# Five more satisfied wait instructions on SyncE ahead of the last store

## The chip, the cores and the metric

The kernel runs on one core of a Trainium2 chip. The metric is the device time of one execution in microseconds (us), lower is better. Each execution also has a span, from the first to the last instruction of the program.

## The reference, cut to what matters

The reference adds a linear-attention block with softmax feature maps and a SiLU feed-forward block, both fed by one layer norm, to their input of 2048 rows and 448 columns:

```python
def reference(A_x, A_wqkv, A_w_phi, A_wo, B_x, B_w1, B_w2):
    ...                                  # _A_ref: attention, _B_ref: SiLU feed-forward
    x = A_x
    xn = _layernorm(x, axis=-1)
    return x + _A_ref(xn, A_wqkv, A_w_phi, A_wo) + _B_ref(xn, B_w1, B_w2)
```

The change touches none of this arithmetic.

## The kernel before

The kernel records all its operations, puts them in order with its own scheduler and then emits each engine's stream. Every finished row tile of the result is stored from ScalarE's queue, except the second half of the very last tile, which SyncE stores. SyncE is the engine that in this program only issues transfers and waits. A wait is an instruction that holds its engine until a semaphore, a counter that engines and transfers raise, has reached a value; it is satisfied if the value was reached before. A store has landed when its data have arrived and its semaphore says so:

```python
P.op("dve", ..., lambda e: e.tensor_tensor(res[:, cs], ob, addend[:, cs], ALU.add), ..., name="out_ev")
P.dma(lambda e: e.dma_start(out=rows_of(out, t, t + 1)[:, 0, cs], in_=res[:, cs]), ..., name="out_dma",
      out_slot=ob_cnt[0] % NOS, eng="sp" if cs.start else "act")
```

This is the loop that emits an engine, SyncE among them. The last lines are SyncE's waits for all stores to have landed (NOS is 4):

```python
def emit_engine(ename, eng):
    waited = {}
    for oid in order[ename]:
        o = ops[oid]
        need = {}
        ...                                  # collects what o depends on
        for key, (sm, val) in need.items():
            if waited.get(key, 0) >= val:
                continue
            eng.wait_ge(sm, val)
            waited[key] = val
        ins = o.fn(eng)
        ...
    if ename == "sp":
        for i in range(NOS):
            if out_cnt[i] > 0:
                eng.wait_ge(out_sems[i], 16 * out_cnt[i])
```

SyncE's stream of the kernel before has 79 instructions. The last five are a transpose issue (75th), the wait for the last addition (76th), the store (77th) and two waits for the landings (78th and 79th).

The softmax here doesn't subtract the row's maximum and nothing guards it: scores larger than these inputs give would overflow.

## Time and profile before

| | before |
|---|---|
| time, first three runs | 149.09, 149.17 and 149.71 us |
| profiled run: time, span | 149.45 us, 147.6 us |
| TensorE busy | 143.4 us, 97% of the span |
| SyncE idle ahead of its last store | 9.5 us |
| last addition done, store issued, end of span | 145.98, 146.07, 147.6 us |

### The profile page before, as it was taken

The page shows a single profiled execution, that of the slowest core. Times are in us where ns is not written, and L with a number is a line of the kernel's source. Part 1 is how long each engine was busy: PE and PEld are TensorE (multiplying, and loading weights), DVE is VectorE, ACT ScalarE, POOL GpSimd, SP SyncE. Part 2 cuts the span into 40 slices and gives each one's busy share as a digit, 9 for nine tenths or more (in the row PEclk, how much of TensorE's full clock was granted, in tenths as well). Part 3 has the DMA queues.
Part 4 walks back from the last instruction along what each step waited for, and adds up shares of the span by engine and source line. Part 5 has one row for each costly group of instructions (what it writes and reads, how often), then busy time and mean ns, then how long its engine had stood idle before and what let it go on. Part 6 is the DMA issues. An engine that isn't in the chain of part 4 may idle for free.

```text
span 147.6 us, 3735 instructions
## 1 busy us (share of the span) xinstructions
PE 143.4 (97%) x1572; PEld 79.7 (54%) x1572; DVE 91.1 (62%) x196; ACT 71.8 (49%) x92; POOL 74.0 (50%) x92
## 2 busy tenths in 40 slices
PE   7989999999999999999999999999999999999994
PEld 7884444544544557655444455555555465555473
DVE  2958997190799889207993018969701958252383
ACT  4657675759994988998655597080000000000000
POOL 8618566501099999996999600983940000000000
PEclk9999999999999999999999999999999999999999
DMA  4999964899920000000387391079676925542154
GB/s 109 331 355 247 295 119 70 154 134 301 334 61 0 0 0 4 4 4 0 41 172 147 77 141 36 0 148 119 127 142 134 232 84 98 107 38 39 34 174 137
DMA packets 44496, 17.53 MB, mean 119 GB/s; under 512 B 37040, under 2 KB 44096, under 8 KB 44480
## 3 DMA queue, kind: packets, MB, share of 16 engines
q1 hardware_dynamic: 41648, 15.10, 50.5%
q10 hardware_dynamic: 2704, 2.17, 4.4%
q8 instruction: 12, 0.20, 0.6%
q0 software_dynamic: 128, 0.03, 0.1%
q14 instruction: 4, 0.03, 0.1%
HBM read 6.57 MB, written 1.84 MB: 57 GB/s over the span
## 4 chain that ended last, share of the span: by engine, by line
PE 92%; DMA 4%; SPq 1%; DVE 1%; issue 1%; ACT 0%
PE psum L482 91%; DMA phT<-in_B_w_dram 4%; SPq L516 1%; DVE x_sb L896 1%; DVE Wqk L636 0%; PE psum L497 0%; ACT last_lo L502 0%; ACT last_hi L502 0%
## 5 line engine op out<-in xcount | busy, mean ns | idle before, releaser
L482 PE MATMUL psum<-xnT,phT 64*128 64x512 bf16 (+1 forms) x428 | 45.6, 350 | 0.9 <-DMA phT<-in_B_w_dram 0.4
L482 PE MATMUL psum<-w_sb,hT 128*128 128x448 bf16 (+1 forms) x238 | 45.4, 341 | 0.0
L814 POOL TENSOR_TENSOR RA<-Ek_sb,Rec 128x896 bf16<-128x896 bf16 x16 | 27.0, 1721 | 13.1 <-DVE Rec L779 10.2
L502 ACT ACTIVATE hT<-psum 128x1024 bf16<-128x1024 f32 x28 | 27.3, 1024 | 12.8 <-PE psum L482 12.8
L778 DVE TENSOR_REDUCE Rec<-Ek_sb 128x32 f32<-128x896 bf16 (+1 forms) x20 | 24.4, 1252 | 14.4 <-POOL Ek_sb L509 7.5
L482 PEld LDWEIGHTS psum<-w_sb,hT 128*128 128x128 bf16 x238 | 22.2, 98 | 18.7 <-issue 1.1
L482 PEld LDWEIGHTS psum<-xnT,phT 64*128 64x128 bf16 (+1 forms) x428 | 21.0, 95 | 20.9 <-PE psum L482 0.6
L502 ACT ACTIVATE Ek_sb<-psum 128x864 bf16<-128x864 f32 x24 | 20.1, 910 | 7.1 <-POOL RA L814 4.4
L482 PE MATMUL psum<-Wqk,xnT 64*128 64x432 bf16 x224 | 23.4, 343 | 0.1
L874 DVE TENSOR_SCALAR den<-psum 128x16 f32<-128x16 f32 x16 | 2.3, 156 | 23.3 <-PE psum L482 23.3
L482 PEld LDWEIGHTS psum<-Wqk,xnT 64*128 64x128 bf16 x224 | 10.5, 94 | 10.1 <-issue 0.8
L788 POOL TENSOR_TENSOR Ek_sb<-Ek_sb,Rec 128x896 bf16<-128x896 bf16 x8 | 13.3, 1700 | 5.1 <-DVE Rec L779 5.1
L788 POOL TENSOR_TENSOR phT<-phT,Rec 128x896 bf16<-128x896 bf16 x8 | 13.3, 1702 | 0.0
L482 PE MATMUL psum<-wv,xnT 64*128 64x448 bf16 x112 | 12.9, 349 | 0.0
L643 DVE BATCH_NORM_STATS2 st<-x_sb 128x6 f32<-128x448 bf16 x16 | 9.6, 603 | 2.9 <-DMA x_sb<-in_A_x_dram 2.9
L482 PE MATMUL psum<-wo_sb,vaug 128*128 128x448 bf16 (+1 forms) x51 | 10.8, 342 | 0.0
L896 DVE TENSOR_TENSOR x_sb<-psum,x_sb 128x448 bf16<-128x448 f32 (+1 forms) x14 | 7.5, 584 | 5.0 <-PE psum L482 5.0
L881 DVE TENSOR_TENSOR vaug<-psum,rden 128x448 bf16<-128x448 f32 x16 | 9.8, 623 | 0.4
L658 DVE TENSOR_SCALAR RA<-x_sb,mv,rstd 128x384 bf16<-128x384 bf16 (+4 forms) x29 | 8.9, 346 | 1.3 <-POOL rstd L654 1.1
L779 DVE RECIPROCAL Rec<-Rec 128x32 f32<-128x32 f32 (+1 forms) x24 | 8.8, 396 | 0.2
L778 DVE TENSOR_REDUCE Rec<-phT 128x64 f32<-128x1792 bf16 x4 | 8.0, 2004 | 0.6 <-ACT phT L502 0.6
L482 PEld LDWEIGHTS psum<-wv,xnT 64*128 64x128 bf16 x112 | 5.5, 94 | 5.2
(59 smaller groups left out, 110.6 us busy)
## 6 DMA issues: line engine op xcount, KB each, us to landing
out_dram<-x_sb ACTq DMA_DIRECT2D x15, 112.0 KB, 1.7
w_sb<-in_B_w_dram SPq DMA_DIRECT2D x1, 1568.0 KB, 8.1
x_sb<-in_A_x_dram SPq DMA_DIRECT2D x3, 448.0 KB, 6.2
wo_sb<-in_A_wo_dram SPq DMA_DIRECT2D x2, 336.0 KB, 7.6
phT<-in_B_w_dram SPq DMA_DIRECT2D x1, 576.0 KB, 7.2
phT<-in_B_w_dram SPq DMA_DIRECT2D x2, 256.0 KB, 4.5
phT<-in_B_w_dram ACTq DMA_DIRECT2D x1, 384.0 KB, 4.8
wv<-in_A_wqkv_dram SPq DMA_DIRECT2D x1, 336.0 KB, 7.3
```

Of the source, the lines that this page charges most:

```text
L482: r = e.matmul(dst, lhsT, rhs, start=st, stop=sp, skip_group_check=True)
L502: P.op("act", d_act(n), lambda e: e.activation(dst, src, func, scale=scale), reads=[src], writes=[dst], table=table, name=name, **keys)
L516: P.dma(lambda e: e.dma_start(out=dst, in_=src), n / 280.0, writes=[dst], name=name, eng=eng, lat=lat)
L643: P.op("dve", 590, lambda e: e.bn_stats(st6[:, t, :], xs), reads=[xs], writes=[st6[:, t, :]], name=f"bnst{t}", okeys_w=["ln"])
L658: P.op("dve", dur, lambda e: e.tensor_scalar(dst, x_sb[:, t, c0:c1], mv[:, t, 0:1], rstd[:, t:t + 1], ALU.subtract, ALU.mult), reads=[xs, ...
L778: P.op("dve", 50 + 967 * n, lambda e: e.tensor_reduce(R2, E4, AXL.X, ALU.add), reads=[E4], writes=[R2], name="Ssum")
L779: P.op("dve", 135 + 210 * n, lambda e: e.reciprocal(R2, R2), reads=[R2], writes=[R2], name="Rrec")
L788: P.op("pool", 1700, lambda e: e.tensor_tensor(E3, E3, Rk[:, :, None].broadcast_to([128, 32, DH]), ALU.mult), reads=[E3, Rk], writes=[E3], ...
L814: P.op("pool", 1700, lambda e: e.tensor_tensor(dst, Eq, Rq.rearrange("p (c j) -> p c j", c=CC)[:, :, :, None].broadcast_to([128, CC, 4, DH ...
L874: P.op("dve", 190, lambda e: e.tensor_scalar(den[:, uq, :], U3[:, :, DH], EPS_DEN, None, ALU.add), reads=[U3[:, :, DH]], writes=[den[:, uq ...
L881: P.op("dve", 620, lambda e: e.tensor_tensor(o3, U3[:, :, 0:DH], rden[:, uq, :, None].broadcast_to([128, H, DH]), ALU.mult), reads=[U3[:, ...
L896: P.op("dve", d_dve(cs.stop - cs.start), lambda e: e.tensor_tensor(res[:, cs], ob, addend[:, cs], ALU.add), reads=[ob, addend[:, cs]], wri ...
```

## The change

The change adds waits on semaphore values that were reached long ago. Its intent is to see what satisfied waits cost on SyncE.

```diff
                     eng.wait_ge(sm, val)
                     waited[key] = val
+                if ename == "sp" and oid == order["sp"][-1]:
+                    for e in ("dve", "act", "pe", "pool", "dve"):
+                        eng.wait_ge(eng_sem[e], 2)
+                        eng.wait_ge(eng_sem[e], 1)
                 ins = o.fn(eng)
```

The builder packs the ten conditions, with the one that blocks, into six wait instructions, so SyncE has 84 instructions instead of 79.

## The prediction

> **What bounds the kernel now.** I read the page from the top: the span, the busy shares, then the chain that ended last.
>
> ```profile
> span 147.6 us, 3735 instructions
> PE 143.4 (97%) x1572; PEld 79.7 (54%) x1572; DVE 91.1 (62%) x196; ACT 71.8 (49%) x92; POOL 74.0 (50%) x92
> ...
> PE 92%; DMA 4%; SPq 1%; DVE 1%; issue 1%; ACT 0%
> ```
>
> The matmul engine is busy in 97% of the span and carries 92% of the chain. The kernel is a long row of matmuls with a short head (the first loads) and a short tail. The change does not touch a matmul or anything that a matmul waits for: it stands just ahead of the very last store. So only the tail has to be read closely. The timeline of the last 3 us (start, length, engine, line, operation):
>
> ```profile
> 145.00 0.45 PE L482 MATMUL psum<-wo_sb,vaug 128*128 128x224 bf16 x3
> 145.19 0.10 PEld L482 LDWEIGHTS psum<-wor_sb,vaug 128*128 128x128 bf16 x1
> 145.20 0.78 DVE L896 TENSOR_TENSOR x_sb<-psum,x_sb 128x224 bf16<-128x224 f32 x2 [0.76 <-PE psum L482]
> 145.29 0.26 PE L482 MATMUL psum<-wor_sb,vaug 128*128 128x224 bf16 x1
> 146.07 0.37 SPq L898 DMA_DIRECT2D out_dram<-x_sb  x1
> ```
>
> The last matmul ends at 145.29 + 0.26 = 145.55, the second of the two VectorE additions at 145.20 + 0.78 = 145.98, and SyncE issues the last half tile at 146.07. That store takes 1.5 us from issue to landing (the list of DMA issues), 146.07 + 1.5 = 147.6, the end of the span. So the tail is serial: matmul, addition, wait of SyncE, issue, landing. Anything put between 145.98 and 146.07 lengthens the kernel by its full length. What decides is whether the five new waits land there. For that I ask how long SyncE stood before this store, and what for (SyncE's own table of waits, over the time after 136 us, and its timeline from 135 us):
>
> ```profile
> SPq L1109 <- DVE x_sb L896: 9.5, 1, 9.5
> SPq L1119 <- DMA out_dram<-x_sb: 1.1, 1, 1.1
> ...
> 135.34 1.19 SPq L583 DMA_TRANSPOSE vaug<-vaug  x1
> 146.07 0.37 SPq L898 DMA_DIRECT2D out_dram<-x_sb  x1
> ```
>
> SyncE's last transpose issue ends at 135.34 + 1.19 = 136.53. From there to 145.98 it has nothing to do: 9.5 us, one single wait, for the VectorE addition. After the store it waits once more, 1.1 us, for landings.
>
> **What the Trainium skill says.** "Perfetto Trace Analysis", section "Identifying Dependency Chains": an instruction that waits on several engines may get separate wait instructions put in front of it that hold the additional conditions. This case agrees: wait instructions stand on the source line of the waits, L1109, 14 of them on SyncE. The same page, section "Sequencer-only Instruction (DRAIN, etc)", says that the profiler records only the execution of such an instruction after its condition is met, and not the waiting. The row agrees with that too:
>
> ```profile
> L1109 SPq EVENT_SEMAPHORE  x1: 17/17/17, 146.0 to 146.0; - x1
> ```
>
> This is the one wait after 136 us, 17 ns long and placed at 146.0, though SyncE had stood there for 9.5 us. The recorded lengths of waits are therefore costs of a satisfied wait, which is what I need here. Third, "Runtime: NRT & Kernel Launch", section "Instruction fetch mechanics": an engine's instructions are refilled in blocks of 16 KiB, 256 instructions, mostly hidden. By that, 84 instead of 79 instructions should cross no further block, unless launch code ahead of them happens to end there; no run so far shows it for this stream.
>
> **The change part by part.** It removes nothing. It adds ten conditions in the source, "at least 2" and "at least 1" for each of five engine names, VectorE named twice. All have long been true: SyncE's last true wait on VectorE in this stretch is for the value 196. The builder packs two conditions into one wait instruction, so the ten become five new instructions, and one condition more rides on the existing wait.
>
> In the source, the new waits stand *after* the loop that emits the true wait for the addition, directly before the store. Read that way, they would all run after 145.98, on the path. But the order of the built instructions on SyncE, which I listed for both kernels, is another one. Before: wait (VectorE at 196), then the store, which itself waits for an early load. After, in this order: wait (TensorE 2); wait (TensorE 1, ScalarE 1); wait (GpSimd 2, ScalarE 2); wait (GpSimd 1, VectorE 1); wait (VectorE 2, VectorE 2); wait (VectorE 1, **VectorE 196**); store. The one condition that blocks has been put into the last of the six, so five satisfied waits stand ahead of it. I built it three times, with the same order each time. On the other engines the order is the same in both kernels.
>
> What does a satisfied wait cost? In the trace SyncE runs transposes back to back, some with one wait instruction between them and some with none:
>
> ```profile
> 120.39 1.19 SPq L583 DMA_TRANSPOSE vaug<-vaug  x1
> 121.62 1.26 SPq L583 DMA_TRANSPOSE vaug<-vaug  x1
> 123.23 1.19 SPq L583 DMA_TRANSPOSE vaug<-vaug  x1
> 124.53 1.20 SPq L583 DMA_TRANSPOSE vaug<-vaug  x1
> 125.83 1.21 SPq L583 DMA_TRANSPOSE vaug<-vaug  x1
> ```
>
> With none, the gap is 121.62 − (120.39 + 1.19) = 0.04 us. With a wait of two conditions (recorded at 28 ns) it is 124.53 − (123.23 + 1.19) = 0.11 us, with a wait of one condition (17 ns) 125.83 − (124.53 + 1.20) = 0.10 us. So one wait adds 0.06 to 0.07 us at the rounding of these rows; I take 0.065 for two conditions and 0.05 for one, because the difference of 28 − 17 = 11 ns in the records has to show.
>
> Five new waits: one of one condition and four of two, 0.05 + 4 × 0.065 = 0.31 us. They start when the last transpose is issued, at 136.53, and are through at 136.84. The addition they give way to ends at 145.98, so 9.1 us of idle time are left and **none of the 0.31 us is on the path**. What is on the path is the one condition that rides on the blocking wait: 11 ns by the records, and possibly nothing, as it may be checked while the other is awaited. Sum: 0.00 to 0.01 us on 149.17, 149.2 after rounding.
>
> **The rivals.** First, source order holds on the chip: the five run after the addition. For it speaks only the text of the source; against it the built order. It would give 149.17 + 0.31 = 149.48 us, 0.2% more, still far within 2%. Second, a wait on an old value is not cheap, or each condition is asked for in a round trip of its own. For it nothing speaks: the 28 ns of the two-condition waits include both; and even 1 us for each of five would fit into 9.5 us. Third, the longer instruction stream costs a fetch. If it fell into the stretch after 136.5 us it would be hidden likewise; only in front of the store itself could it hurt, by an unknown amount, and the quiet 9.5 us before it leave the fetching all the time it wants. Fourth, the transposes' issue moves and with it TensorE. Against it: the new waits stand behind all transposes in SyncE's order, so nothing earlier can see them.
>
> **Range and chances.** The kernel's own scatter is larger than any of this: its three runs spread over 149.09 to 149.71, 0.6 us, and the first rival's 0.31 us lies inside it. So the middle is 149.2, and the range 148.9 to 149.6 is mostly the scatter of a median of a few runs, with some room above for the first rival. For 2% it would take 3.0 us, ten times the full price of the five waits when fully exposed. Nothing is removed, so a real gain is as unlikely: 0.01 for each side.
>
> **What would show it right or wrong.** In SyncE's timeline after the change, the last transpose should be issued at about 135.3 and end at 136.5; five wait records of 17 to 28 ns should stand within 0.4 us after it, and only one, now of 28 ns rather than 17, at about 146.0. SyncE's wait for the addition should read 9.5 − 0.3 = 9.2 us. The store should start 0.09 to 0.10 us after the addition ends, as before (146.07 − 145.98 = 0.09), and all matmul rows should be unchanged. The prediction of the mechanism is wrong if the five stand between the addition and the store and that gap reads about 0.4 us; it is wrong altogether if the store's landing or the head of the kernel moves, which nothing in the change explains.

## More of the kernel before

The time is longer than the span, because what stands before the program's first instruction and after its last one counts in the time and not in the span. That difference is called "time outside the span" here, and it turned out to carry this case.

## The result, and the profile after

| | before | changed |
|---|---|---|
| time, median | 149.44 us (6 runs, 149.09 to 153.31) | 148.60 us (6 runs, 148.42 to 148.78) |
| profiled run: time, span | 149.45, 147.6 us | 148.72, 147.5 us |
| time outside the span, profiled run | 1.85 us | 1.22 us |

The ratio is 0.9946 with a 95% interval of 0.9920 to 0.9972. Ratios here are the mean time of one kernel's fast runs over that of the other's of the same rounds, so they are not quite the ratios of the medians quoted beside them; the run of 153.31 us was slow and is not in it. The kernel became faster by about 0.5%, where the prediction had no gain at all, and 148.60 lies below its range of 148.9 to 149.6.

The tail inside the span is nearly what it was. The timeline of the changed kernel's last microseconds (start, length, engine, line, operation):

```profile
145.08 0.77 DVE L896 TENSOR_TENSOR x_sb<-psum,x_sb 128x224 bf16<-128x224 f32 x2 [0.76 <-PE psum L482]
145.17 0.26 PE L482 MATMUL psum<-wor_sb,vaug 128*128 128x224 bf16 x1
145.92 0.36 SPq L898 DMA_DIRECT2D out_dram<-x_sb  x1
```

The addition ends at 145.08 + 0.77 = 145.85, or 145.858 by the trace's own times, and the store follows 0.06 us later, at 145.92, against 0.09 us before. So the five waits are not between them. All of this is 0.13 us earlier than before. The first loads, at the head of the chain, took 5.04 us instead of 5.22 us, more than enough for it; the change stands far behind them, and this figure lies between 5.00 and 5.54 us in the other runs.

Where the waits went is in the rows of the lines that emit them, L1113 and L1114. The rows below were asked for in two stretches of time, up to 137.1 us and from 137.1 us on (line, engine, operation, count, shortest, median and longest ns, first and last start):

```profile
L1113 SPq EVENT_SEMAPHORE  x2: 17/22/28, 136.5 to 136.6; - x2
L1114 SPq EVENT_SEMAPHORE  x2: 28/28/28, 136.5 to 136.7; - x2
...
L1113 SPq EVENT_SEMAPHORE  x1: 28/28/28, 137.2 to 137.2; - x1
L1114 SPq EVENT_SEMAPHORE  x1: 8641/8641/8641, 137.2 to 137.2; - x1
```

SyncE's table of waits after 136 us, in the same kernel:

```profile
SPq L1114 <- DVE x_sb L896: 8.7, 1, 8.7
```

Four of the new waits start at 136.47, 136.53, 136.60 and 136.67 us, 0.07 us apart, as predicted. The fifth, SyncE's 80th instruction, starts at 137.17 us, 0.50 us after the fourth. It ought to have come 0.07 us after it, so SyncE stood still for 0.43 us. SyncE's wait for the addition reads 8.7 us instead of the predicted 9.2 us, and nearly all of the missing 0.5 us is this stop. It is harmless there, because SyncE would have waited anyway. But a stop that nobody waits for cannot make a kernel faster by itself; the question is where it was in the kernel before.

The list of DMA queues answers that. Queue q14 carries instructions. The rows of the whole page, before first and changed second (packets, MB, share):

```profile
q14 instruction: 4, 0.03, 0.1%
```

```profile
q14 instruction: 5, 0.04, 0.1%
```

The changed kernel fetches one block of instructions more inside its span. In the trace it is a packet of 8,192 bytes at 137.80 us, 0.63 us after the stop ended. The list for the changed kernel from 137 to 139 us has it as this row:

```profile
q14 instruction: 1, 0.01, 1.7%
```

Was the fetch absent before? The same list for the kernel before, over the stretch from 148 to 149 us, that is after its span had ended at 147.63 us, says:

```profile
DMA packets 1, 0.01 MB, mean 8 GB/s; under 512 B 0, under 2 KB 0, under 8 KB 0
...
q14 instruction: 1, 0.01, 2.8%
```

There it is, at 148.72 us by the trace, after the last instruction of the program. The changed kernel has no such packet after its span. If the fetch follows the stop by 0.63 us here too, the stop ended at 148.09 us and, being some 0.45 us long, began right at 147.63 us, where SyncE's 79th and last instruction ended. This is an estimate from the two traces. The later runs bear the 0.63 us out: in again, n1, n3, n4, early1 and nos2tail the packet starts 0.61 to 0.68 us after the 80th instruction, in n2 0.92 us. The estimate gave the theory for the experiments.

### The profile page after: what moved, and what is told of

Read it like the earlier page. It is cut to its first block, busy times and chain, and to the rows that moved or that the text cites. A ratio compares the mean times of both kernels' runs of the same rounds, so it can differ in the third digit from the quotient of the medians.

```text
span 147.5 us, 3740 instructions
## 1 busy us (share of the span) xinstructions
PE 143.5 (97%) x1572; PEld 79.9 (54%) x1572; DVE 91.1 (62%) x196; ACT 71.8 (49%) x92; POOL 74.1 (50%) x92
## 4 chain that ended last, share of the span: by engine, by line
PE 92%; DMA 3%; SPq 1%; DVE 1%; issue 1%; ACT 0%
PE psum L482 92%; DMA phT<-in_B_w_dram 3%; SPq L516 1%; DVE x_sb L896 1%; DVE Wqk L636 1%; PE psum L497 0%; ACT last_lo L502 0%; ACT last_hi L502 0%
```

## The experiments

**Refill theory.** Between its 79th and its 80th instruction SyncE stops for about 0.45 us, because it has to ask for a new block of instructions there. With 79 instructions the stop comes right after the program's end and is paid in full. With 84 it falls into idle time. **Rivals:** the waits themselves save something; a blocking wait that carries two conditions is released sooner; additional instructions on any engine change the end; or the gain is chance.

A drain, which some of the runs use, serves only as one instruction more that moves no data.

In each run I read the time outside the span beside the time, because each of the timed runs has both. It scatters by only about 0.1 us, while the span of the kernel before scatters by 1 us and more. The runs of one call shared a chip and the runs of the kernel before: n1, n3, nos2tail and cond1 one set of 11, the others a second set of 11 or 12. In both sets the kernel before had a median of 1.78 us outside the span (1.74 to 1.86 and 1.73 to 1.81). All results were correct. The second set holds one run of 150.97 us, with a granted clock of 0.989, which lowers the ratios to it somewhat and widens their intervals; the time outside the span is not touched by it.

| run | SyncE instructions | what the 80th is | outside the span, median | span, mean (of before) | ratio to before (interval) |
|---|---|---|---|---|---|
| nos2 | 78 | after the program | 1.67 us | 147.60 (147.66) us | 0.9986 (0.9950 to 1.0021) |
| cond1 | 79 | after the program | 1.76 us | 147.95 (147.74) us | 1.0012 (0.9988 to 1.0036) |
| act5 | 79 | after the program | 1.80 us | 147.55 (147.62) us | 0.9990 (0.9956 to 1.0025) |
| n1 | 80 | second wait for the landings | 1.28 us | 147.62 (147.74) us | 0.9958 (0.9934 to 0.9981) |
| early1 | 80 | second wait for the landings | 1.28 us | 147.43 (147.66) us | 0.9948 (0.9913 to 0.9983) |
| n2 | 81 | first wait for the landings | 1.27 us | 147.57 (147.62) us | 0.9960 (0.9923 to 0.9997) |
| n3 | 82 | the last store | 1.25 us | 148.62 (147.74) us | 1.0021 (0.9997 to 1.0046) |
| nos2tail | 82 | a drain after the landings | 1.24 us | 148.58 (147.74) us | 1.0021 (0.9998 to 1.0044) |
| n4 | 83 | the blocking wait | 1.27 us | 147.63 (147.66) us | 0.9959 (0.9922 to 0.9997) |
| again | 84 | the fifth new wait | 1.24 us | 147.42 (147.66) us | 0.9945 (0.9908 to 0.9981) |

Two things in the traces go with this table. It is where the stop falls that counts, and not where the fetched block moves: in n1, n2, early1 and nos2tail the packet too starts after the span's end, by 0.2 to 0.4 us, and they have 1.24 to 1.28 us outside the span. In before, cond1, act5 and nos2 it starts 1.09 to 1.13 us after the end. And the difference of 0.53 us outside the span is some 0.1 us more than the stop, which is 0.41 to 0.43 us longer than the usual gap wherever a trace shows it by itself (after, again, n2, n3, n4, nos2tail). No run says where the rest comes from.

### n1: one wait instruction more

```diff
+                if ename == "sp" and oid == order["sp"][-1]:
+                    for n in range(2):
+                        eng.wait_ge(eng_sem[("dve", "act", "pe", "pool")[n // 2 % 4]], 2 - n % 2)
                 ins = o.fn(eng)
```

> One wait instruction more ahead of the last store, 80 instead of 79 on SyncE. Refill theory (SyncE stands about 0.45 us between its 79th and 80th instruction, because a new block of instructions has to be asked for there; in the kernel before this comes after the last instruction and lengthens the time, in the changed kernel it falls into idle time): here the 80th is the last wait for the landings, which takes 1.1 us anyway, so the stop is hidden and the time is 0.5 to 0.8 us below before, as with five waits. Rival 'the waits themselves help' (each of five saves something): about a fifth, 0.1 to 0.2 us. Rival 'chance' (both kernels equal): ratio 1.000 within its interval.

The median was 148.90 us against 149.56 us. Outside the span it was 1.28 us, 0.50 us less than before. One wait gives what five give, so a saving per wait falls. In the profiled run the last wait for the landings starts 0.73 us after the one ahead of it has ended, against 0.72 us in the kernel before: it is held up by a landing either way. The stop can't be seen by itself there; that it is hidden follows from the time outside the span.

### n3: three wait instructions more

```diff
-                    for n in range(2):
+                    for n in range(6):
```

(The lines taken away here and in the diffs of cond1, n4 and n2 are those of n1.)

> Three wait instructions more, 82 on SyncE. The 79th is now the blocking wait for the last addition and the 80th the store. Refill theory: if the stop comes only when the 80th is reached, the store starts 0.5 us after the addition ends instead of 0.09 us, the span grows by 0.4 us to about 148.0, and the time is about that of before (within 0.2 us), not faster. If the block is asked for some instructions ahead, the stop is hidden and the time is as with five waits, 0.6 us below before. Rival 'the waits themselves help': about 0.4 us below before. Rival 'chance': equal to before, but with the store 0.09 us after the addition.

The median was 149.90 us against 149.56 us. The first reading of the theory held: nothing is asked for ahead, the stop comes when the 80th instruction is reached. The timeline of this run:

```profile
145.35 0.78 DVE L896 TENSOR_TENSOR x_sb<-psum,x_sb 128x224 bf16<-128x224 f32 x2 [0.75 <-PE psum L482]
...
146.62 0.36 SPq L898 DMA_DIRECT2D out_dram<-x_sb  x1
```

Its list of issues after 146 us (size, time from issue to landing):

```profile
out_dram<-x_sb SPq DMA_DIRECT2D x1, 56.0 KB, 2.1
```

The addition ends at 145.35 + 0.78 = 146.13 and the store starts at 146.62, 0.49 us later instead of 0.09 us. The second view holds something I had not expected: the store takes 2.1 us to land instead of 1.5 us. The fetched block moved at 147.29 to 147.89 us and the store's own data at 147.47 to 148.06 us, so they overlapped. The data took 0.59 us to move instead of 0.34 us. By the trace, 135 of the store's 144 packets have ended by 147.82 us, and the last nine, one sixteenth of them, start only from 147.88 us on, when the fetched block has moved; so one of the 16 DMA engines seems to have carried the block first. The sum fits: 0.40 us for the stop and 0.53 us for the landing (2.09 − 1.57 by the trace) make 0.93 us, the mean span grew by 148.62 − 147.74 = 0.88 us, and with 0.53 us less outside the span 0.35 us are left. The means differ by 149.87 − 149.52 = 0.35 us. The expected span of 148.0 us was too short by the landing.

### nos2tail: one wait less, four drains at the very end

```diff
-        NOS = 4
+        NOS = 2
 ...
                         eng.wait_ge(out_sems[i], 16 * out_cnt[i])
+                for n in range(4):
+                    eng.drain()
```

> No new wait ahead of the store; two output semaphores instead of four (one wait less), and four drains at the end, the first of them carrying the last wait for the landings as 79th instruction, three more after it as 80th to 82nd. Refill theory: the stop of about 0.45 us, which lies unseen after the end in the kernel before, becomes visible between the 79th and the 80th; the span grows by about 0.5 us plus three drains of some 0.05 us, and the time is before's or up to 0.2 us more. Rival 'waits help' and 'chance': no stop between the drains; span and time grow by at most 0.2 us, all of it in the drains.

This run lets the stop be seen where the kernel before has it, behind the last landing. The drains' rows, asked for up to 148 us and from 148 us on (columns as above):

```profile
L1121 SPq DRAIN  x1: 13/13/13, 147.8 to 147.8; - x1
...
L1121 SPq DRAIN  x3: 7/7/109, 148.3 to 148.5; - x3
```

The first drain, the 79th instruction, ends at 147.80 us when the last store has landed. The 80th starts at 148.27 us. A drain has nothing to wait for there, and the gap is 0.47 us, where the next two drains follow after 0.05 us each. Of the time outside the span 0.54 us went into the span, which became 0.84 us longer by the means: 0.70 us of it are the stop and the three drains in the trace, of which one took 0.11 us. The rest is within the scatter of the span. The time grew by 0.3 us by the means, a little more than the expected 0.2 us at most.

### cond1: the blocking wait with two conditions, 79 instructions

```diff
-                    for n in range(2):
+                    for n in range(1):
```

> 79 instructions as before, but the blocking wait carries one satisfied condition more, as it does in the changed kernel. Refill theory: time as before within 0.1 us, at most 0.02 us less because the store starts 0.07 instead of 0.09 us after the addition. Rival 'the two-condition wait is released sooner and that is the gain': 0.5 us or more below before. Rival 'chance': as before.

The median was 149.70 us against 149.56 us, with 1.76 us outside the span. A second condition on the blocking wait gains nothing that these runs can show. The store came 0.08 us after the addition. This rival falls.

### again: the changed kernel once more

> The changed kernel once more. Time outside the span (time of a run less its span, every run has both): 1.25 us as in its first runs, against 1.78 us of before, so 0.53 us less. The refill theory says that only this difference belongs to the change: 0.53 us of 149.5 is a ratio of 0.9965; the span itself should then be equal to before's within its scatter of 0.5 us, and the 0.3 us by which its span was shorter the first time should be gone or have the other sign. If the waits also shorten the span, it is again 0.3 us or more below before's.

The median was 148.57 us against 149.20 us. Outside the span it was 1.24 against 1.78 us, 0.54 us less. The spans' medians are 147.35 and 147.40 us, equal for this purpose; the means differ by 0.24 us, because one run of the kernel before had a span of 149.2 us; without it they differ by 0.09 us. So the ratio of 0.9945 contains a part that is scatter: what belongs to the change is 0.54 us of 149.2, a ratio of 0.9964, which lies inside the interval. Chance falls too: the changed kernel's twelve runs have 1.22 to 1.29 us outside the span, the 23 runs of the kernel before in the two sets 1.73 to 1.86 us.

### early1: one drain at 37 us

```diff
+                if ename == "sp" and o.name == "wor1":
+                    eng.drain()
                 for key, (sm, val) in need.items():
```

> No wait added; one drain, at 36 us, ahead of the fifth-to-last early load, where SyncE has nothing to do for 35 us. 80 instructions on SyncE. Refill theory: the place of the added instruction does not matter, only that the 80th is inside the kernel and in a stretch where SyncE waits anyway; here it is the last wait for the landings. Time outside the span 1.25 us, time 0.5 us below before. If what helps are waits on old values just ahead of the last store, the time is before's and 1.78 us lie outside the span.

The drain in fact stands at 37.49 us, ahead of the last of the early loads, which does not matter here. The median was 148.72 us against 149.20 us, with 1.28 us outside the span. The instruction need not be a wait, and it need not stand near the end. What counts in these runs is how many instructions SyncE has, and so which of them is the 80th.

### nos2: one instruction fewer

```diff
-        NOS = 4
+        NOS = 2
```

> One instruction fewer than before, 78 on SyncE (two output semaphores instead of four, so one final wait). Refill theory: the stop comes still after the end of the kernel, one instruction later in what follows it; time outside the span 1.7 to 1.8 us, time as before within 0.1 us. If simply fewer or other instructions at the end were what counts, it would be faster than before.

The median was 149.22 us against 149.20 us. Outside the span it was 1.67 us, somewhat below the expected 1.7 us to 1.8 us, and below all runs of the kernel before. The fetch came after the span, at 148.54 us. The stop is still paid when it comes one instruction later, but the price is 0.11 us less: 1.67 us is 0.42 us above the 1.25 us of the runs without it, the length of the stop itself. Why it costs 0.53 us directly after the last instruction is open; I did not look into what follows the program.

### n4: four wait instructions more

```diff
-                    for n in range(2):
+                    for n in range(8):
```

> Four wait instructions more, 83 on SyncE: the 80th is the blocking wait for the addition itself. Refill theory: the stop lies between the fourth new wait and the blocking wait, at 136.9 to 137.4 us, within the idle time; store 0.07 us after the addition, outside the span 1.25 us, time 0.5 us below before. That is one instruction more than the run with three, which was 0.3 us above before: a cost of the number of waits would have to rise smoothly, the stop jumps.

The median was 148.94 us against 149.20 us, with 1.27 us outside the span. Line L1113 in this run, the waits that start up to 137 us and the one after:

```profile
L1113 SPq EVENT_SEMAPHORE  x4: 17/28/28, 136.7 to 136.9; - x4
...
L1113 SPq EVENT_SEMAPHORE  x1: 8733/8733/8733, 137.4 to 137.4; - x1
```

The stop now stands between the fourth new wait, at 136.90 us, and the blocking wait, at 137.39 us. From three to four waits the ratio falls from 1.0021 to 0.9959. A cost per wait could not do that.

### n2: two wait instructions more

```diff
-                    for n in range(2):
+                    for n in range(4):
```

> Two wait instructions more, 81 on SyncE: the stop falls between the store and the first of the two waits for the landings. Refill theory: the stop itself is hidden, because the landing takes 1.5 us from the store's issue; outside the span 1.25 us; store 0.07 to 0.09 us after the addition. What is open is the fetched block: it moves some 0.6 us after the stop, in the run with three it fell into the store's own data and the landing took 2.1 instead of 1.57 us. Here it would move at about 1.4 us after the store's issue, just past the data (0.86 to 1.2 us after it): landing 1.6 us and time 0.5 us below before; if it still meets the data, landing up to 2.1 us and the time equal to before.

The median was 148.88 us against 149.19 us. The store was issued at 145.67 us for 0.37 us, and the first wait for the landings started at 146.51 us, so the stop is seen between them, as a gap of 0.47 us. The row of the two waits for the landings:

```profile
L1122 SPq EVENT_SEMAPHORE  x2: 28/212/395, 146.5 to 146.8; - x2
```

The fetch moved at 147.42 us, after the store's data (146.54 to 146.87 us), some 0.35 us later than I expected, and the landing took 1.57 us. Together with the nine late packets of n3 this speaks for the meeting of fetch and data as the cause of the long landing there. It was not tried by itself, and why the fetch came later here is open.

### act5: five drains on ScalarE

```diff
+                if ename == "act" and oid == order["act"][-1]:
+                    for n in range(5):
+                        eng.drain()
                 for key, (sm, val) in need.items():
```

> Five drains on ScalarE ahead of its last store, in 0.8 us in which it waits anyway; SyncE has 79 as before. Refill theory: nothing changes, 1.78 us outside the span, time as before within 0.15 us. If additional instructions on any engine changed what follows the kernel, the time outside the span would differ from 1.78 us.

The median was 149.34 us against 149.19 us, with 1.80 us outside the span. Five instructions more on ScalarE change nothing beyond the scatter; the other engines were not tried.

## Why the prediction was right or wrong

The prediction of 149.2 us was wrong by 0.6 us, and its reading of the waits was right.

- **What bounds the kernel, and where the waits run.** Right. The matmuls are unchanged (143.5 us busy), and the built order was kept: four waits within 0.3 us after the last transpose, the fifth after the stop, none between the addition and the store.
- **The cost of the waits.** Right in size, but not in its signs. 0.065 us was predicted for a wait of two conditions and 0.07 us was measured. Up to the start of the blocking wait the five took 137.25 − 136.47 = 0.78 us; less the stop of 0.43 us this is 0.35 us, where 0.31 us were expected. It is hidden. Two of the records that it named as signs were different: the five waits were not within 0.4 us after the transpose (the fifth started 0.76 us after it, because of the stop), and the blocking wait was recorded as 8,641 ns from 137.25 us on and not as 28 ns at 146.0 us. So the step that all recorded lengths of waits are costs of satisfied waits was wrong; the trace before already had a wait of 5,199 ns on SyncE, at 90.6 us.
- **The condition on the blocking wait.** Its 0.01 us cannot be seen. In cond1, which has it alone, the store came 0.08 us after the addition, in the changed kernel 0.06 us.
- **The third rival, a fetch.** This is the step that failed. The prediction said that a fetch would be hidden in the idle time, which is right, and that "only in front of the store itself could it hurt". It hurts in two places: in front of the store (n3), and behind the program's last instruction, where the kernel before already paid for it. The hedge "unless launch code ahead of them happens to end there" named the very case and was then put aside. A cost that already existed was asked for only as a cost that might be added. The blocks of 256 instructions that it reckoned with were not met either: SyncE's packet has 8,192 bytes, and the stop comes after the program's 79th instruction. So the possible sign of this rival was wrong: a longer stream pulled the stop from the exposed end into idle time and took 0.53 us off. Shown is a stop that is bound to SyncE's 80th instruction and an instruction packet that follows it; that the stop is the asking for that block is argued from this order, and in the kernel before itself the stop is estimated and not seen.
- **The end of the kernel.** Under this lies a tacit step: that the path ends with the span. The prediction had 149.45 us and 147.6 us before it and did not ask what the 1.85 us between them were.
- **The range.** It was drawn from the scatter of the time alone, and a real shift of 0.53 us from a middle of 149.2 falls out of it below. The chances (0.98 for within 2%) were right.

Of the first ratio, 0.9946, the shift outside the span explains 0.53 us, or 0.36%. The remainder is luck, scatter of the span, as the run again shows by its medians.

No run here beats the changed kernel outside the span: all runs whose stop is hidden lie at 1.24 to 1.28 us. The cheapest way to the same gain is one single instruction more (n1 or early1).

## What to carry to other kernels

Take the time less the span as a row of its own, in the kernel before and after, for what follows the last instruction is on the path too: here 0.53 us of it could be saved. Where a change adds or removes instructions on the engine that ends last, look in the instruction queue of the DMA list for a fetch near or after the end: here one instruction more moved its stop into a wait (n1), and two more again put it in front of the last store (n3). A gain of this kind belongs to the count of instructions and not to what they do, so it can be lost with the next edit.

## What the Trainium skill lacked or had wrong

- "Runtime: NRT & Kernel Launch", section "Instruction fetch mechanics", calls the cost of crossing a block's boundary one DMA tail-bump, "mostly hidden", and gives no size. SyncE stood 0.41 to 0.43 us longer than usual at each stop seen by itself here (in the changed kernel 0.50 us from wait to wait instead of 0.07 us), and where nothing hid it (n3) the store came 0.40 us later. The page does not say that a crossing can fall behind a program's last instruction and count in its time: 1.78 us outside the span with it, 1.25 us without. That these stops are such crossings is argued from the packet that follows each.
- The same page gives refills of 16 KiB, 256 instructions, for the engines. SyncE's packet here was 8,192 bytes; other packets in the same traces have 16,384 bytes. With the 64-byte instructions of "Perfetto Trace Analysis", section "The 4-stage abstract model", 8,192 bytes are 128 instructions, so a crossing after the program's 79th would leave 49 ahead of the program. That is an estimate; no run shows those.
- No page gives a figure for what a fetched block costs a store that it meets. In n3 it moved beside the store's data, nine of the 144 packets came after it, and the landing took 2.09 us instead of 1.57 us.
- "Perfetto Trace Analysis", section "Sequencer-only Instruction (DRAIN, etc)", has the recorded start when all conditions are met. A wait with two conditions, one of them long met, was recorded from its own beginning: 8,641 ns in the changed kernel, against 17 ns for the blocking wait with a single condition before.
